# Windowed attention and a tanh-shrink MLP on one core: a new order of loads, gates set tile by tile, and global-row copies for the freer engine

## The chip, the core and the metric

The kernel runs on one core of a Trainium2 chip. The core has a matrix engine (TensorE, PE in the profile), a vector engine (VectorE, DVE), an activation engine (ScalarE, ACT), a general engine (GpSimd, POOL) and a sync engine (SyncE, SP). Each works through its own list of instructions in order; semaphores hold an instruction back until what it needs is there. Transfers between memories are issued by POOL, SP or ACT and carried out by sixteen transfer engines. The metric is the device time of one execution in microseconds (us).

## The reference

Inputs are q, k, v of shape (4, 8, 768, 64) and two weights, `moe_w_in` (512, 2048) and `moe_w_out` (2048, 512), all float32.

```
scores = q @ k^T / sqrt(64)
keep   = (key < 8) | (0 <= query - key < 96)
bias   = -slope[h] * (96 if global and not local else |query - key|)
a      = softmax(where(keep, scores + bias, -1e9))
x      = (a @ v), heads put side by side     -> (3072, 512)
h      = x @ w_in
out    = (h - tanh(h)) @ w_out               -> (3072, 512)
```

So each query sees at most 96 keys behind it and the first 8 keys of its batch, the global rows.

## The kernel before

**Tiles.** The 3072 rows are 24 units u of 128 rows, six to a batch. A unit needs the keys of its own block and of the block before it (`blocks(u)`), so the eight global rows lie outside these for units 2 to 5 of a batch. The kernel copies the global rows of K and V over the first eight rows of the preceding block's tile (rows that the window doesn't reach): `a_K` copies 8 columns of the transposed K tile, `a_V` 8 rows of the V tile. In the kernel before, VectorE makes all of these copies.

**Steps of a unit.** Load q and k (`lq`, `lk`) and v (`lv`); transpose q and k: on PE for u below 8 (`T`, then copies `Te` out of PSUM), by a transposing DMA on SP from u = 8 on (also `T`); scores `S` (PE); exp `E` (ACT); mask by multiplication `M` (DVE); `AV` (PE); division by the sum `R` (DVE); transpose of the result, `X` and `Xe`, again on PE below 8 and by SP's DMA above.

**Groups of the MLP.** Units 0 and 1 are groups of their own, the others go in pairs (2, 3), (4, 5) and so on, 13 groups g. `m1(g, f)` multiplies blocks of 128 columns of w_in, from block f on, with the group's transposed activations: four blocks for a single, two for a pair, so that a task fills one PSUM bank. `th` is the tanh on ACT, `g` the subtraction on DVE. The second layer is `m2` for units 0 to 3. For the pairs from unit 4 on, the product of two row blocks with two halves of w_out is made with seven products `p` in place of eight, on sums and differences of the inputs (`wm`, `gm`); `kp` and `jn` copy and add the results, `st` stores them.

**Weights.** w_in comes in five loads, in0 to in4, that end at column blocks 2, 4, 8, 12 and 16 (`in_end`), each in a tile of its own, w_in_bf0 to w_in_bf4. w_out comes in four loads, out0 to out3.

**What sets the order.** The kernel first writes down every step as a task with its engine (or engines: the freer one at that moment gets it), an estimated duration, what it must come after, the buffers it takes and gives, and a priority. A small planner (`Plan.run`) plays this through and yields each engine's order; only then the instructions are written in that order. The semaphores are set afterwards from the data that each instruction really reads and writes, not from the planner's list. `NUDGE` holds additions to the priorities of single tasks. `order` is a string that gives the order of the loads on POOL's queue; each load is planned after the one before it. `AHEAD` and `T_AHEAD`, both 6.0, are gates: `S(u)` and `T(u)` may not be planned before the MLP tasks have come to within six units of u. For m1 the planner's list has these lines:

```python
op(("m1", g, f), PE, ..., after=[("Xe", u) for u in us] + [("in", in_of[f + m - 1]), ...
# in m1: for f in range(f0, f0 + m): j = in_of[f]; ... w_in_bf[j] ...
```

In the profile of before, L517 is m1's matmul, L589 a product, L542 m2, L449 S, L475 AV, L405 and L417 the transposes of q and k, L495 that of the result, L369 the bias, L871 warming matmuls on zeros; L388 and L391 load q, k and v, L394 loads w_in, L397 w_out; L605 stores.

Of the kernel before, what the change touches and what calls it, by code (L numbers as in the profile page):

```python
# [11 lines left out]
ALU = mybir.AluOpType  # L12
# [186 lines left out]
def kernel(  # L199
# [41 lines left out]
    WM_PRI = 40  # L241

    groups = [[u] for u in range(SINGLE)] + [[u, u + 1] for u in range(SINGLE, NU, 2)]
    group_of = {u: g for g, us in enumerate(groups) for u in us}
    seven = [g for g, us in enumerate(groups) if SEVEN[0] <= us[0] < SEVEN[1]]
# [35 lines left out]
    buffers("pr", 5, [P, H, P], BF16)  # L281
    buffers("x", 3, [P, H, Dh], BF16)
    buffers("xT", 4, [P, CD, 2 * P], BF16)
    buffers("th", 4, [P, 512], FP32)
    buffers("g", 4, [P, CF, 2 * P], BF16)
# [5 lines left out]
    def buf(holder, j=0):  # L291
# [23 lines left out]
    def slot(h):  # L315
        return (h % 2) * NP + h // 2
# [137 lines left out]
    def a_E(u, o):  # L454
        d = buf(("p", u, o)).rearrange("k (a h) f -> k a (h f)", a=2)
        nc.scalar.activation(d, banks(("s", u), 2 * o, 2 * o + 1), AF.Exp, bias=0.0, scale=scale)  # L456

    def a_M(u, o):
        t = buf(("p", u, o))
        nc.vector.tensor_tensor(out=t, in0=t, in1=mk[:, mask_of(u, o)], op=ALU.mult)  # L460
# [10 lines left out]
    def a_AV(u):  # L471
        t = av(u)
        for h in range(H):
            for o in blocks(u):
                nc.tensor.matmul(  # L475
                    t[:, h // (H // 2), h % (H // 2), :], buf(("p", u, o))[:, slot(h), :], buf(("v", u - o))[:, h, :],
                    start=o == 0, stop=o == blocks(u)[-1],
                )
# [30 lines left out]
    def m1(g, f0, m):  # L509
        n = len(groups[g]) * P  # L510
        t = bank(("h", g, f0))
        x = buf(("xT", g))
        for f in range(f0, f0 + m):
            j = in_of[f]
            fo = (f - in_from[j]) * P
            for c in range(CD):
                nc.tensor.matmul(  # L517
                    t[:, (f - f0) * n : (f - f0 + 1) * n], w_in_bf[j][:, c, fo : fo + P], x[:, c, 0:n],
                    start=(c == 0), stop=(c == CD - 1),
                )  # L520
# [4 lines left out]

    def m1_th(g, f0, m):
        nc.scalar.activation(  # L527
            h_view(buf(("th", g, f0)), g, m), h_view(bank(("h", g, f0)), g, m), AF.Tanh, bias=0.0, scale=1.0
        )

    def m1_g(g, f0, m):
        n = len(groups[g]) * P
        nc.vector.tensor_tensor(  # L533
            out=buf(("g", g))[:, f0 : f0 + m, 0:n], in0=h_view(bank(("h", g, f0)), g, m),
            in1=h_view(buf(("th", g, f0)), g, m), op=ALU.subtract,
        )

    def m2(u, part, fs, c0, c1):
        g = group_of[u]
        t = groups[g].index(u)  # L540
        for f in fs:
            nc.tensor.matmul(  # L542
                bank(part)[:, 0 : c1 - c0], buf(("g", g))[:, f, t * P : (t + 1) * P],
                w_out_bf[:, f, c0:c1], start=(f == 0), stop=(f == CF - 1),
            )
# [20 lines left out]
    def w_mixes(i):  # L566
        t = [w_mix[:, n] for n in range(4)]
        if i == 0:
            sub(t[0], w_half(0, 1), w_half(0, 0))
        elif i == 1:  # L570
            sub(t[1], w_half(1, 1), t[0])
        elif i == 2:
            sub(t[2], w_half(1, 1), w_half(0, 1))
        else:
            sub(t[3], w_half(1, 0), t[1])
# [46 lines left out]
    T_AHEAD = 6.0  # L622
# [23 lines left out]
    for u in range(HW):  # L646
# [16 lines left out]
    )  # L663
    ring = [(x.rstrip("0123456789"), int(x.lstrip("kqvinout"))) for x in order.split()]
    prev = None
    for kind, u in ring:
        if kind == "v":
# [14 lines left out]
        elif kind == "in":  # L682
            load(("in", u), POOL, 0.75, lambda e, u=u: load_w_in(e, u), W_WT * (in_end[u] - in_from[u]) / 4, prev, pri=-40)
            prev = ("in", u)
        else:
            load(("out", u), POOL, 0.75, lambda e, u=u: load_w_out(e, u), W_WT, prev, pri=-40)
            prev = ("out", u)

# [3 lines left out]
    for g, us in enumerate(groups):  # L692
        m = 4 // len(us)
        units[g] = [(f, m) for f in range(0, CF, m)]
        for f, m in units[g]:
            prog.append((acc, ("m1", g, f)))
            acc += len(us) * m / CF

    FLEX = (ACT, DVE)
    for u in range(NU):  # L700
# [3 lines left out]
        go = [key for a, key in prog if a <= u - AHEAD]  # L704
        here = [("ck", u), ("cq", u)] if u < HW else [("lk", u), ("lq", u)]
        first = [key for a, key in prog if a <= u - T_AHEAD]
        tdep = here + [("issue", first[-1]) if first else None]
        sdep = [("issue", go[-1])] if go else []
# [26 lines left out]
        for o in blocks(u):  # L735
            op(("E", u, o), ACT, 1.03, lambda e, u=u, o=o: a_E(u, o), after=[("S", u)],
               take=[(("p", u, o), "pr", 1)], give=[(("s", u), (2 * o, 2 * o + 1))], pri=base)
            if u >= BIASED:
# [8 lines left out]
        a_give = [(("p", u, o), None) for o in blocks(u)]  # L747
# [23 lines left out]
    for g, us in enumerate(groups):  # L771
        n = len(us) * P
        for f, m in units[g]:
# [4 lines left out]
               take=[(("h", g, f), "bank", 1)], pri=pri,  # L778
# [3 lines left out]
               take=[(("th", g, f), "th", 1)], pri=pri)  # L782
            op(("g", g, f), DVE, 0.15 + 1.07 * w, lambda e, g=g, f=f, m=m: m1_g(g, f, m),
               after=[("th", g, f), ("issue", ("g", g, 0)) if f else None],
               take=[(("g", g), "g", 1)] if f == 0 else [], give=[(("h", g, f), None), (("th", g, f), None)], pri=pri)
# [8 lines left out]
    for i in range(4):  # L794
        op(("wm", i), DVE, 0.15 + 2048 / 1920, lambda e, i=i: w_mixes(i),
           after=[("out", j) for j in range(WJ)] + ([("wm", i - 1)] if i in (1, 3) else []) + ([("wm", 1)] if i == 3 else []), pri=WM_PRI)
    for g, us in enumerate(groups):
        if g not in seven:
            continue
        u0, u1 = us  # L800
        pri = 1030 + 10.0 * u0
        done = [("g", g, f) for f, m in units[g]]
# [13 lines left out]
        prod(6, sa, lambda g=g: mix(g, 1), lambda: w_mix[:, 1], False, [("gm", g, 1), ("wm", 1), ("kp", g, 0)], [], mg)  # L816
        prod(5, sb, lambda g=g: mix(g, 0), lambda: w_mix[:, 0], True, [("gm", g, 0), ("wm", 0), ("jn", g, 0)], [], mg)
        prod(7, sa, lambda g=g: mix(g, 2), lambda: w_mix[:, 2], False, [("gm", g, 2), ("wm", 2), ("kp", g, 1)], [], mg)
        prod(4, sa, lambda g=g: g_half(g, 1, 1), lambda: w_mix[:, 3], False, [("wm", 3), ("kp", g, 2)], [], gg)
# [19 lines left out]
    for u in range(NU):  # L839
        g = group_of[u]  # L840
        if g in seven:
            continue
# [3 lines left out]
        for c0, c1 in cols:  # L846
            part = ("o", u, c0)
            steps = [range(4 * a, 4 * a + 4) for a in range(4)] if c1 - c0 == DM else [range(CF)]
            for a, fs in enumerate(steps):
                op(("m2", u, c0, a), PE, len(fs) * ((c1 - c0) / 2400.0 + 0.0025),  # L850
                   lambda e, u=u, part=part, fs=fs, c0=c0, c1=c1: m2(u, part, fs, c0, c1),
                   after=[("out", fs[-1] // FJ), ("issue", prev) if prev else None] + [("g", g, f) for f in sorted({f // m * m for f in fs})],
                   take=[(part, "bank", 1)] if a == 0 else [],
                   give=[(("g", g), None)] if a == len(steps) - 1 else [],
# [6 lines left out]
            wait = ("p", group_of[u + 1], 1) if u + 1 < NU and group_of[u + 1] in seven else ("m2", u + 1, 0, 2)  # L861
# [61 lines left out]
```

## Time and profile before

| | before |
|---|---|
| time, median of 3 runs | 209.36 us (208.21 to 210.05) |
| profiled execution, first to last instruction (its span) | 207.0 us |
| PE busy | 200.6 us, 97% |
| DVE busy | 164.7 us, 80% |
| ACT busy | 123.4 us, 60% |
| POOL busy | 79.6 us, 38% |
| mean granted clock of PE | 0.997 |
| moved by the transfer engines | 26.85 MB |

The span runs from the first to the last instruction of one profiled execution; for that execution no other time is recorded, so its own time is this span and what lies around it, and the median of the runs is 2.4 us above the span. Busy time is the time in which an engine has an instruction under way. Idle time matters only on the engine that others wait for. A row of groups gives line, engine, operation, tiles, shapes and count, then busy time and the mean of one in ns, then the idle time just before and what ended it.

### The profile page before, as it was taken

What the parts mean: (1) busy time and instruction counts of PE and PEld (TensorE: products, weight loads), DVE (VectorE), ACT (ScalarE), POOL (GpSimd) and SP (SyncE); (2) the same over time, 40 slices, a digit from 0 to 9 for tenths busy, and PEclk for the clock granted to TensorE, in tenths of its full rate; (3) what the DMA queues carried; (4) which work ended last, traced back from release to release, by engine and by line L of the source; (5) the groups of instructions that cost most, each with busy time, mean ns of one, the idle gap of its engine ahead of it and who ended that gap; (6) DMA issues with size and microseconds to landing.
All of it is one profiled execution on the core that took longest, in us unless ns stands there. A gap on an engine that the chain in (4) does not pass through costs nothing.

```text
span 207.0 us, 5642 instructions
## 1 busy us (share of the span) xinstructions
PE 200.6 (97%) x2303; PEld 165.9 (80%) x2303; DVE 164.7 (80%) x336; ACT 123.4 (60%) x194; POOL 79.6 (38%) x105
## 2 busy tenths in 40 slices
PE   5998999999999998999999999999999999999993
PEld 1568987758668887888889888888898898888883
DVE  5339995898689897898988998888899889775761
ACT  3698966456747685556577545756656745545320
POOL 7997336498465543536391732002101020000030
PEclk9999999999999999999999999999999999999998
DMA  5999999999999999999999999922462022000052
GB/s 134 148 168 197 207 190 189 177 157 145 133 157 190 147 181 113 167 166 157 119 213 131 233 119 157 189 48 101 85 139 63 0 76 79 0 3 0 3 209 98
DMA packets 101514, 26.85 MB, mean 130 GB/s; under 512 B 92848, under 2 KB 100016, under 8 KB 101488
## 3 DMA queue, kind: packets, MB, share of 16 engines
q0 software_dynamic: 74624, 18.88, 94.9%
q1 hardware_dynamic: 26592, 7.34, 26.5%
q8 instruction: 18, 0.29, 0.6%
q10 hardware_dynamic: 272, 0.26, 0.5%
q14 instruction: 8, 0.07, 0.1%
HBM read 27.26 MB, written 6.29 MB: 162 GB/s over the span
## 4 chain that ended last, share of the span: by engine, by line
PE 91%; DMA 4%; DVE 2%; POOL 1%; issue 1%; POOLq 0%; DVEq 0%
PE ps L517 38%; PE ps L589 29%; PE ps L542 7%; PE ps L449 6%; PE ps L475 5%; DMA xT<-x 4%; PE ps L369 2%; PE ps L417 1%; PE ps L495 1%; PE ps L405 1%; DVE x L484 1%; DVE slopes L359 0%; PE ps L413 0%; POOL kq L388 0%; DVE ot L596 0%
## 5 line engine op out<-in xcount | busy, mean ns | idle before, releaser
L517 PE MATMUL ps<-xT,w_in_bf 128*128 128x256 bf16 (+1 forms) x832 | 92.8, 264 | 0.6 <-DMA xT<-x 0.6
L517 PEld LDWEIGHTS <-w_in_bf 128*128 128x128 bf16 x832 | 74.8, 98 | 9.5 <-issue 0.8
L527 ACT ACTIVATE th<-ps 128x512 f32<-128x512 f32 x96 | 56.9, 600 | 42.4 <-PE ps L517 39.3
L533 DVE TENSOR_TENSOR g<-ps,th 128x512 bf16<-128x512 f32 x96 | 62.8, 682 | 8.5 <-ACT th L527 7.8
L456 ACT ACTIVATE pr<-ps 128x1024 bf16<-128x1024 f32 x44 | 43.5, 1027 | 6.3 <-PE ps L449 6.2
L605 POOL DMA_DIRECT2D out_dram<-ot x21 | 11.8, 562 | 78.8 <-DVE ot L596 36.3
L589 PEld LDWEIGHTS <-mix 128*128 128x128 bf16 x320 | 30.7, 98 | 4.1
L589 PE MATMUL ps<-w_mix,mix 128*128 128x256 bf16 x240 | 29.7, 273 | 0.0
L460 DVE TENSOR_TENSOR pr<-pr,mk 128x1024 bf16<-128x1024 bf16 x39 | 26.2, 681 | 1.9 <-ACT pr L456 1.7
L589 PEld LDWEIGHTS <-g 128*128 128x128 bf16 x240 | 22.9, 98 | 3.3
L391 POOL DMA_DIRECT2D vb<-in_v_dram x24 | 21.3, 894 | 10.4 <-DVE pr L460 3.6
L391 POOL DMA_DIRECT2D kq<-in_k_dram x20 | 17.8, 888 | 17.2 <-DMA qk<-kq 9.1
L391 POOL DMA_DIRECT2D kq<-in_q_dram x20 | 17.8, 888 | 6.9 <-DMA kq<-in_q_dram 2.7
L589 PE MATMUL ps<-w_out_bf,g 128*128 128x256 bf16 x160 | 20.0, 273 | 0.0
L596 DVE TENSOR_TENSOR ot<-ps,part 128x256 f32<-128x256 f32 x30 | 12.7, 422 | 7.5 <-PE ps L589 5.3
L323 ACT COPY part<-ps 128x256 f32<-128x256 f32 x25 | 9.3, 372 | 15.3 <-PE ps L589 15.2
L484 DVE TENSOR_TENSOR x<-ps,rden 128x512 bf16<-128x512 f32 x24 | 16.6, 692 | 0.8
L542 PE MATMUL ps<-w_out_bf,g 128*128 128x512 bf16 x64 | 16.0, 379 | 0.0
L475 PE MATMUL ps<-vb,pr 128*128 128x65 bf16 x352 | 14.6, 193 | 0.0
L475 PEld LDWEIGHTS <-pr 128*128 128x128 bf16 x352 | 13.7, 97 | 1.0
L449 PEld LDWEIGHTS <-qk 64*128 64x128 bf16 x352 | 9.9, 94 | 5.4 <-issue 4.6
L564 DVE TENSOR_TENSOR mix<-g 128x1024 bf16<-128x1024 bf16 x20 | 13.6, 681 | 0.0
(57 smaller groups left out, 147.7 us busy)
## 6 DMA issues: line engine op xcount, KB each, us to landing
out_dram<-ot POOLq DMA_DIRECT2D x21, 256.0 KB, 6.4
vb<-in_v_dram POOLq DMA_DIRECT2D x24, 128.0 KB, 11.1
kq<-in_k_dram POOLq DMA_DIRECT2D x23, 128.0 KB, 9.9
kq<-in_q_dram POOLq DMA_DIRECT2D x23, 128.0 KB, 10.2
w_out_bf<-in_moe_w_out_dram POOLq DMA_DIRECT2D x4, 512.0 KB, 14.0
w_in_bf<-in_moe_w_in_dram POOLq DMA_DIRECT2D x3, 512.0 KB, 9.6
w_in_bf<-in_moe_w_in_dram POOLq DMA_DIRECT2D x2, 256.0 KB, 6.2
out_dram<-ot SPq DMA_DIRECT2D x4, 128.0 KB, 1.7
```

Of the source, the lines that this page charges most:

```text
L391: eng(e).dma_start(out=dst, in_=rows_of(src, u).rearrange("h p d -> p h d"))
L449: nc.tensor.matmul(bank(("s", u), 2 * o + hh)[:, p * P : (p + 1) * P], buf(("qk", u - o))[r, 1, p, :], buf(("qk", u))[r, 0, p, :], start=u ...
L456: nc.scalar.activation(d, banks(("s", u), 2 * o, 2 * o + 1), AF.Exp, bias=0.0, scale=scale)
L460: nc.vector.tensor_tensor(out=t, in0=t, in1=mk[:, mask_of(u, o)], op=ALU.mult)
L475: nc.tensor.matmul(t[:, h // (H // 2), h % (H // 2), :], buf(("p", u, o))[:, slot(h), :], buf(("v", u - o))[:, h, :], start=o == 0, stop=o ...
L484: nc.vector.tensor_tensor(out=buf(("x", u)).rearrange("q (a h) d -> q a h d", a=2), in0=t[:, :, :, 0:Dh], in1=rden.to_broadcast([P, 2, H / ...
L517: nc.tensor.matmul(t[:, (f - f0) * n : (f - f0 + 1) * n], w_in_bf[j][:, c, fo : fo + P], x[:, c, 0:n], start=(c == 0), stop=(c == CD - 1),)
L527: nc.scalar.activation(h_view(buf(("th", g, f0)), g, m), h_view(bank(("h", g, f0)), g, m), AF.Tanh, bias=0.0, scale=1.0)
L533: nc.vector.tensor_tensor(out=buf(("g", g))[:, f0 : f0 + m, 0:n], in0=h_view(bank(("h", g, f0)), g, m), in1=h_view(buf(("th", g, f0)), g, ...
L542: nc.tensor.matmul(bank(part)[:, 0 : c1 - c0], buf(("g", g))[:, f, t * P : (t + 1) * P], w_out_bf[:, f, c0:c1], start=(f == 0), stop=(f == ...
L564: nc.vector.tensor_tensor(out=out, in0=a, in1=b, op=op)
L589: nc.tensor.matmul(bank(part)[:, 0:NH], a[:, j], w[:, j], start=first and j == 0, stop=j == CF // 2 - 1, skip_group_check=not first)
```

## The change

The computation stays the same. What changes:

- `COPIES = (DVE, ACT)`: the planner may give each `K` and `V` copy to VectorE or to ScalarE.
- `GATE`: the number of units by which `S(u)` and `T(u)` keep behind the MLP is given for each u from 6 on, in place of 6.0 for all.
- `order`: the loads are put in a new order; among others in1, in3 and in4 come ahead of in0, and in2 after it.
- `NUDGE`: some 60 priorities become about 190.
- Tasks of the product pairs are numbered by u // 2; tiles `pr` have one more dimension of size 1. Some switches are new and off (`WIDE`, `JOINED`, `WH = 1`) and change nothing.

```diff
+    COPIES = (DVE, ACT)
...
     NUDGE = {
-        ('rel',): 850, ('dist',): 2630, ('lq', 1): 4260, ('lk', 12): 1980, ('S', 0): 910, ('AV', 0): 2360,
...
+        ('rel',): 850, ('dist',): -1670, ('first',): 1500, ('turn',): 4500, ('bm', 0): -2100, ('ck', 0): 7100,
...
-    T_AHEAD = 6.0
+    GATE = {
+        ('T', 6): 3.5, ('S', 6): 3.5, ('T', 7): 1.25, ('S', 7): 2.25, ('T', 8): 3, ('S', 8): 5.25, ('T', 9): 4.5,
...
     order = (
-        "kq1 kq2 in0 v0 v1 v2 kq3 v3 kq4 in1 in2 in3 in4 out0 kq5 out1 v4 v5 out2 out3 kq6 v6 kq7 kq8 "
-        "kq9 v7 v8 v9 kq10 v10 kq11 kq12 v11 v12 v13 kq13 kq14 v14 v15 kq15 kq16 v16 kq17 v17 kq18 "
-        "v18 kq19 v19 kq20 v20 kq21 kq22 v21 v22 v23 kq23 "
+        "kq1 v0 kq3 kq2 v1 in1 in3 v3 v2 in4 kq5 in0 kq4 in2 out1 out0 v4 kq6 out2 out3 kq7 v5 kq8 v7 v6 kq9 "
+        "kq10 v23 kq12 kq11 v8 v10 v9 v16 v12 kq14 v13 kq13 kq15 v11 kq20 kq16 v19 v14 v18 v21 kq22 v15 v22 "
+        "kq17 v20 kq23 v17 kq18 kq21 kq19 "
     )
...
-        go = [key for a, key in prog if a <= u - AHEAD]
+        ga = sum(a <= GATE.get(("S", u), u - AHEAD) for a, _ in prog) - 1
+        gt = sum(a <= GATE.get(("T", u), u - AHEAD) for a, _ in prog) - 1
...
-            op(("K", u), DVE, 0.16, lambda e, u=u: a_K(e, u), after=[("S", u)],
+            op(("K", u), COPIES, 0.17, lambda e, u=u: a_K(e, u), us2=0.25, after=[("S", u)],
-            op(("V", u), DVE, 0.3, lambda e, u=u: a_V(e, u), after=[("AV", u)],
+            op(("V", u), COPIES, 0.3, lambda e, u=u: a_V(e, u), us2=0.62, after=[("AV", u)],
```

In the program that comes of it, the first tasks on PE are, before: bm1, B0, bm2, T0, bm0, T1, T2, S0, B1, S1, B2, S2, AV0, AV1, T3, X1, X0, AV2, S3, T4, X2, m1(0, 0), m1(1, 0); after: bm1, bm0, B0, bm2, T0, T1, S0, B1, S1, AV0, T3, T2, X0, B2, AV1, S2, m1(0, 0), X1, S3, m1(0, 8), m1(1, 0), AV2.

More of the change, by code (lines that the diff above doesn't have):

```diff
@@ L241 @@
     WM_PRI = 40
+    WH = 1
+    WIDE = {}
+    COPIES = (DVE, ACT)
+    JOINED = False
     groups = [[u] for u in range(SINGLE)] + [[u, u + 1] for u in range(SINGLE, NU, 2)]
     group_of = {u: g for g, us in enumerate(groups) for u in us}
-    seven = [g for g, us in enumerate(groups) if SEVEN[0] <= us[0] < SEVEN[1]]
+    seven = [w for w in range(NU // 2) if SEVEN[0] <= 2 * w < SEVEN[1]]
     pool = ctx.enter_context(tc.tile_pool(name="sb", bufs=1))
@@ L533, in m1_g @@
         nc.vector.tensor_tensor(
-            out=buf(("g", g))[:, f0 : f0 + m, 0:n], in0=h_view(bank(("h", g, f0)), g, m),
+            out=g_cols(groups[g][0], n)[:, f0 : f0 + m], in0=h_banks(g, f0, m),
             in1=h_view(buf(("th", g, f0)), g, m), op=ALU.subtract,
@@ L564, in sub, with w_mixes @@
         nc.vector.tensor_tensor(out=out, in0=a, in1=b, op=op)
-    def w_mixes(i):
-        t = [w_mix[:, n] for n in range(4)]
+    def w_mixes(i, j):
+        c = slice(j * CF // (2 * WH), (j + 1) * CF // (2 * WH))
+        t = [w_mix[:, n, c] for n in range(4)]
         if i == 0:
-            sub(t[0], w_half(0, 1), w_half(0, 0))
+            sub(t[0], w_half(0, 1)[:, c], w_half(0, 0)[:, c])
         elif i == 1:
-            sub(t[1], w_half(1, 1), t[0])
+            sub(t[1], w_half(1, 1)[:, c], t[0])
         elif i == 2:
-            sub(t[2], w_half(1, 1), w_half(0, 1))
+            sub(t[2], w_half(1, 1)[:, c], w_half(0, 1)[:, c])
         else:
-            sub(t[3], w_half(1, 0), t[1])
+            sub(t[3], w_half(1, 0)[:, c], t[1])
     def g_mixes(g, i):
@@ L665 @@
     prev = None
+    plan.chain = []
     for kind, u in ring:
+        first = len(plan.ops)
         if kind == "v":
@@ L687 @@
             prev = ("out", u)
+        plan.chain.append(list(plan.ops)[first:])
     units = {}
@@ L692 @@
     for g, us in enumerate(groups):
-        m = 4 // len(us)
-        units[g] = [(f, m) for f in range(0, CF, m)]
+        sizes = WIDE.get(g, [4 // len(us)] * (CF * len(us) // 4))
+        units[g] = [(sum(sizes[:i]), m) for i, m in enumerate(sizes)]
         for f, m in units[g]:
@@ L697 @@
             acc += len(us) * m / CF
-    FLEX = (ACT, DVE)
+    plan.prog = [key for a, key in prog]
+    plan.accs = [a for a, key in prog]
+    plan.gates = {}
     for u in range(NU):
@@ L703 @@
         base = 10.0 * u
-        go = [key for a, key in prog if a <= u - AHEAD]
+        ga = sum(a <= GATE.get(("S", u), u - AHEAD) for a, _ in prog) - 1
+        gt = sum(a <= GATE.get(("T", u), u - AHEAD) for a, _ in prog) - 1
         here = [("ck", u), ("cq", u)] if u < HW else [("lk", u), ("lq", u)]
-        first = [key for a, key in prog if a <= u - T_AHEAD]
-        tdep = here + [("issue", first[-1]) if first else None]
-        sdep = [("issue", go[-1])] if go else []
+        tdep = here + [("issue", prog[gt][1]) if gt >= 0 else None]
+        sdep = [("issue", prog[ga][1])] if ga >= 0 else []
+        if gt >= 0:
+            plan.gates["T", u] = gt
+        if ga >= 0:
+            plan.gates["S", u] = ga
         kq_give = [(("kq", u), None)]
@@ L735 @@
         for o in blocks(u):
-            op(("E", u, o), ACT, 1.03, lambda e, u=u, o=o: a_E(u, o), after=[("S", u)],
-               take=[(("p", u, o), "pr", 1)], give=[(("s", u), (2 * o, 2 * o + 1))], pri=base)
-            if u >= BIASED:
+            op(("E", u, o), ACT, 1.03, lambda e, u=u, o=o: a_E(u, o), after=[("S", u)] + ([("issue", ("E", u, 0))] if JOINED and o else []),
+               take=[] if JOINED and o else [(("p", u), "pr", 1)] if JOINED else [(("p", u, o), "pr", 1)],
+               give=[(("s", u), (2 * o, 2 * o + 1))], pri=base)
+            if u >= BIASED and JOINED and nb == 2:
+                if o:
+                    op(("M", u), DVE, 1.22, lambda e, u=u: a_M2(u),
+                       after=[("E", u, 0), ("E", u, 1), ("em", 1), ("em", 2)], pri=base)
+            elif u >= BIASED:
                 op(("M", u, o), DVE, 0.71, lambda e, u=u, o=o: a_M(u, o),
@@ L794, with wmd @@
     for i in range(4):
[L795 to L800, printed above, removed]
+        for j in range(WH):
+            op(("wm", i, j), DVE, 0.15 + 2048 / WH / 1920, lambda e, i=i, j=j: w_mixes(i, j),
+               after=[("out", n) for n in range(j * WJ // WH, (j + 1) * WJ // WH)]
+               + ([("wm", i - 1, j)] if i in (1, 3) else []) + ([("wm", 1, j)] if i == 3 else []), pri=WM_PRI)
+    def wmd(i):
+        return [("wm", i, j) for j in range(WH)]
+    for g in seven:
+        u0, u1 = 2 * g, 2 * g + 1
         pri = 1030 + 10.0 * u0
-        done = [("g", g, f) for f, m in units[g]]
+        done = [("g", h, f) for h in sorted({group_of[u0], group_of[u1]}) for f, m in units[h]]
         for i in range(4):
@@ L840 @@
         g = group_of[u]
-        if g in seven:
+        if u // 2 in seven:
             continue
@@ L851 @@
                    lambda e, u=u, part=part, fs=fs, c0=c0, c1=c1: m2(u, part, fs, c0, c1),
-                   after=[("out", fs[-1] // FJ), ("issue", prev) if prev else None] + [("g", g, f) for f in sorted({f // m * m for f in fs})],
+                   after=[("out", fs[-1] // FJ), ("issue", prev) if prev else None] + [("g", g, f) for f, m in units[g] if f <= fs[-1] and f + m > fs[0]],
                    take=[(part, "bank", 1)] if a == 0 else [],
-                   give=[(("g", g), None)] if a == len(steps) - 1 else [],
+                   give=[(("g", u // 2), None)] if a == len(steps) - 1 else [],
                    pri=1030 + 10.0 * u)
```

55 lines of the change are left out of this document (35 added, 20 removed), and 45 rows, old and new, of tables (GATE, NUDGE).

## The prediction

> **What bounds the kernel now.** I read the page first: busy times, the slices, the queues.
>
> ```profile
> span 207.0 us, 5642 instructions
> PE 200.6 (97%) x2303; PEld 165.9 (80%) x2303; DVE 164.7 (80%) x336; ACT 123.4 (60%) x194; POOL 79.6 (38%) x105
> ...
> DMA  5999999999999999999999999922462022000052
> ...
> q0 software_dynamic: 74624, 18.88, 94.9%
> ```
>
> TensorE (PE) is busy for 97% of the span. The transfer engines are full from the second slice to the twenty-sixth, about 134 us: POOL's queue q0 always has a backlog there. A busy PE need not be a PE at work, so next the busy time by stretch: the start, the stretch from the first matmul of the first MLP layer on, and the end.
>
> ```profile
> 4.80:19.40 14.60, 13.99 (x189) 9.28 (x190) 7.67 (x30) 11.31 (x14) 14.29 (x18) 1.00 1.69 168
> 19.40:203.90 184.50, 183.83 (x2112) 155.93 (x2108) 154.40 (x294) 110.19 (x179) 61.72 (x79) 1.00 1.22 127
> 203.90:207.00 3.10, 0.00 (x0) 0.00 (x0) 0.39 (x1) 0.00 (x0) 0.00 (x0) 0.82 0.25 85
> ```
>
> The columns are length, then PE, PEld, DVE, ACT and POOL busy, clock, DMA share, GB/s. From 19.4 us to 203.9 us PE lacks 0.7 us of 184.5; behind it lie 3.1 us, the last sum and stores. The table of waits names the 0.6 us of it, one wait for a transposed activation:
>
> ```profile
> PE ps L517 <- DMA xT<-x: 0.6, 1, 0.6
> ```
>
> So the kernel is PE from end to end. A reordering can win back little, since each matmul stays; what it can do is make PE wait, and then the end moves by the whole wait. The question for each part is therefore: what does PE now wait for that it did not?
>
> **The change part by part.** *The order of the loads.* The old order issues the five pieces of w_in as in0, in1, in2, in3, in4; the new one issues in1, in3, v3, v2, in4, kq5, in0, kq4, in2. Piece in0 holds column blocks 0 and 1, in1 blocks 2 and 3. The planner lets the task m1(g, f) wait for the piece of its last block alone (`in_of[f + m - 1]`). For the single groups m is 4, so m1(0, 0) multiplies with blocks 0 to 3 and needs in0 and in1, but is planned on in1 only. In the old order that is harmless, since in0 lands first. In the new program m1(0, 0) is the 17th task on PE, its first weight load reads in0, and in0 is the 16th load on POOL's queue. The real semaphore is there whatever the planner thinks, and PE works strictly in its order: all of PE stands until in0 has landed.
>
> When does it land? POOL's issues of before (start, length), and the loads' times from issue to landing:
>
> ```profile
> 9.54 0.89 POOL L391 DMA_DIRECT2D vb<-in_v_dram  x1
> ...
> 11.28 0.89 POOL L391 DMA_DIRECT2D kq<-in_q_dram  x1
> 12.15 1.61 POOL L394 DMA_DIRECT2D w_in_bf<-in_moe_w_in_dram  x2
> 13.92 1.48 POOL L394 DMA_DIRECT2D w_in_bf<-in_moe_w_in_dram  x2 [0.15 <-issue]
> 15.38 0.76 POOL L397 DMA_DIRECT2D w_out_bf<-in_moe_w_out_dram  x1
> ...
> 17.01 0.89 POOL L391 DMA_DIRECT2D kq<-in_q_dram  x1
> ```
>
> ```profile
> kq<-in_k_dram POOLq DMA_DIRECT2D x1, 128.0 KB, 4.1
> ...
> vb<-in_v_dram POOLq DMA_DIRECT2D x1, 128.0 KB, 6.0
> ...
> kq<-in_q_dram POOLq DMA_DIRECT2D x1, 128.0 KB, 5.8
> ...
> w_in_bf<-in_moe_w_in_dram POOLq DMA_DIRECT2D x1, 256.0 KB, 6.3
> ...
> w_in_bf<-in_moe_w_in_dram POOLq DMA_DIRECT2D x1, 512.0 KB, 8.0
> ...
> w_out_bf<-in_moe_w_out_dram POOLq DMA_DIRECT2D x1, 512.0 KB, 14.0
> ...
> kq<-in_q_dram POOLq DMA_DIRECT2D x1, 128.0 KB, 14.0
> ```
>
> ```profile
> DMA to landing us min/median/max: 6.0/8.0/12.1
> ```
>
> The first of these lists is POOL's timeline, the second the list of issues, asked around single ones in the order of issue (the first is the very first load, on an empty queue), the third the answer on the five w_in loads: in0, the first, has the shortest time, in4, the last, the longest. Issue and landing added: v3 (9.5) is in at 15.5, q4 (11.3) at 17.1, in1 (12.15) at 18.4, in2 (13.0, the second of its row) at 21.0, in4 (14.65, the second of its row) at 26.7, the first piece of w_out (15.4) at 29.4, q5 (17.0) at 31.0. The issues are 0.9 us apart and the time to landing grows from 6 to 14 us: the loads come in one behind the other, in the order of issue, and what a load costs is the step to the one before it: in2 2.6, k4 with q4 1.6, k5 with q5 1.6.
>
> In the old order 17 loads end with in4, at 26.7. In the new one 16 loads end with in0: the same without in2 and kq4, and with kq5. So in0 lands at 26.7 - 2.6 - 1.6 + 1.6 = 24.1 us; I take 24.2, for the iota that now stands ahead of the first load (below). The bounds: 18.0 us if in0 needed only the very first load's 4.1 us after the 16th issue, which began at 13.9 in the old order; 25.5 if the iota's whole time and a slower mix shift it. The growing landing times speak for the queue, near the upper end.
>
> A sentence of the Trainium skill speaks for the lower end: "DMA: Bandwidth & Descriptors", section "Anatomy of one DMA — SWDGE (gpsimd) path", gives 2.0 us plus the bytes over 436 GB/s. By it the 3.1 MB that these 16 loads write would be in an estimated 9.2 us after the first issue, PE would not wait at all, and the sum would stay near 207. The rows differ: in2's 512 KB took 2.6 us, about 200 GB/s, and the rows decide.
>
> *When PE gets there, and how much is behind.* Old PE work ahead of m1(0, 0) that the new order puts behind it: X1, AV2, S3, T4, X2. From the chain of work (start, length):
>
> ```profile
> 17.11 0.55 PE ps L495 x8
> 17.67 0.48 PE ps L475 x16
> 18.15 0.55 PE ps L449 x16
> 18.71 0.55 PE ps L405 x8
> 19.26 0.32 PE ps L495 x4
> ```
>
> Half of the first row, and the other four: 2.2 us. So PE reaches m1(0, 0) at 19.4 - 2.2 = 17.2 us at the latest, and waits some 7 us; it can be 15, if the constants come earlier. How early does not matter. From the landing on PE has the old 184.5 us (the 0.6 us wait left in) plus 2.2: 24.2 + 184.5 + 2.2 = 210.9 us.
>
> *The clock.* The trace has PE idle for long only at its end, and cold only at its start:
>
> ```profile
> 200.00:205.80 5.80, 3.82 (x36) 3.18 (x33) 1.27 (x3) 0.74 (x2) 0.00 (x0) 1.00 0.45 159
> 205.90:207.00 1.10, 0.00 (x0) 0.00 (x0) 0.00 (x0) 0.00 (x0) 0.00 (x0) 0.50 0.00 0
> ```
>
> ```profile
> 4.88 2.74 PE ps L369 x6
> ...
> 8.92 0.43 PE ps L369 x2
> ```
>
> ```profile
> L871 PE MATMUL ps<-zero 128*128 128x512 bf16 x7 | 3.4, 627 | 1.0 <-DVE vb L365 1.0
> ```
>
> The granted clock falls from 1.00 to 0.50 about 2 us after the last matmul. At the start the 512-column matmul takes 0.46 us at 4.9 us and 0.22 at 8.9: PE's first, warming matmuls had begun after 1.0 us of idling, so the half clock lasts about 7 us. A wait of 7 us is over three times the 2 us, so I expect the clock to fall and matmuls to go at half speed after the wait. That costs half of the slow time: 0 if the clock does not fall, 3.5 if all 7 us come again. I take 2.4, nearer the upper end, as at the start PE was also idle for part of the time. The Trainium skill says the same in "TensorE: Matmul & The Clock Gate", "What's actually happening": half clock after an idle window of 3.4 us, full again after a busy one; with free-running windows that is 3.4 to 6.8 slow us, an estimated loss of 1.7 to 3.4.
>
> *Copies of the global rows.* Counting the new order, 14 of the 16 V copies and 5 of the 16 K copies go to ScalarE.
>
> ```profile
> L325 DVE COPY vb<-vb 8x512 bf16<-8x512 bf16 x16 | 6.1, 380 | 0.8 <-PE ps L475 0.8
> L325 DVE COPY qk<-qk 128x32 bf16<-128x32 bf16 x16 | 3.3, 208 | 3.3 <-PE ps L449 3.3
> L323 ACT COPY part<-ps 128x256 f32<-128x256 f32 x25 | 9.3, 372 | 15.3 <-PE ps L589 15.2
> L323 ACT COPY xT<-ps 128x512 bf16<-128x512 bf16 x5 | 2.9, 587 | 1.4 <-PE ps L495 1.4
> ```
>
> VectorE loses 14 x 0.38 + 5 x 0.21 = 6.4 us. ScalarE gains 19 copies; this copy has no row there, so 0.2 (VectorE's K copy) to 0.59 each, 4 to 11 us; I take 0.5, as 512 elements a row is the V copy's form, about 9 us on 123. Neither is on the path: PE lacks 0.7 us in all, so relief on VectorE buys nothing, and ScalarE is idle 40% of the span. With that cover gone, an exp or tanh behind a copy is 0.5 us late, and so may PE be: 0 to +2 over the kernel; I take 0.
>
> *Gates, priorities, later loads.* The same matmuls in another order: 0 by itself. Eight matmuls of m1 or of a product take 0.87 us:
>
> ```profile
> 85.15 1.75 PE ps L589 x16
> 86.90 1.75 PE ps L517 x16
> ```
>
> By these, S's 0.55 and AV's 0.48 I counted along both orders the PE work between the last AV of a pair and its first m1, which must hide the SP transposes: for g = 5, where the 0.6 us wait was, it goes from 8.8 to 8.4 us, so the wait may be 1.0; for g = 9 from 10.3 to 7.6, for g = 11 from 18.7 to 8.0. Between S and the AV of the same u it stays at 4.4 us or more from u = 4 on. Loads have 7 us more lead on a PE that is late. -0.6 to +2; I take 0. The two warming matmuls fewer and the constants (iota ahead of the first load, dist ahead of slopes) move PE's start, which the wait swallows.
>
> *The end.* The stores of rows 20 and 21 come two products ahead of the end instead of six. From the list of issues:
>
> ```profile
> out_dram<-ot POOLq DMA_DIRECT2D x21, 256.0 KB, 6.4
> ...
> out_dram<-ot SPq DMA_DIRECT2D x1, 256.0 KB, 3.7
> ```
>
> Store 20, on POOL, is issued about 1.2 us ahead of PE's end. At SP's 3.7 us it lands 2.5 after it, inside the 3.1; at the median 6.4, which has the loads beside it, 5.2 after it: 0 to +2.1; I take 0, as the loads are done by then.
>
> *The sum.* 210.9 + 2.4 = 213.3 for PE's end, + 3.1 = 216.4 us of span against 207.0: +9.4. The runs' median, 209.36, lies 2.4 us above that span, which I keep: 218.8 us.
>
> **The rivals.** (1) The wait comes, but the clock stays up. For it: nothing in the trace shows a fall followed by work. Against: the 0.50 after 2 us of idling. 216.4 us. (2) The wait comes and more follows: late exps behind copies, transposes with less cover, the last POOL store. For it: the shorter covers for g = 9 and 11. Against: PE was fed without a gap with covers as short. With the upper ends (+2, +2, and half the cold time more), 221 to 224 us. (3) Not slower: loads on the queue do not wait for each other, and in0 lands as the first load on an empty queue does, 4.1 us after its issue, at 18.0. PE waits 1 to 3 us, the clock stays: 18.0 + 184.5 + 2.2 + 3.1 + 2.4 = 210.2 us, within 1% of before. It decides from a landing at 19.2 us or earlier (211.4 us). For it: in0 took 6.0 us in the old order with four loads ahead, not much more than 4.1. Against: the growing landing times. (4) The change does not do what it says, because PE is not really held at m1(0, 0): only if in0's weight load stood later; the program's order has it first.
>
> **How the numbers follow.** Forecast 0.74; (1) 0.10; (2) 0.12; (3) 0.03; (4) 0.01. The forecast's own range, with in0 from 23.7 to 25 and the clock term from 1.5 to 3.4, is 217.4 to 220.6. With (1) below, its landing as uncertain, and most of (2) above: 215.0 to 223.3. A measurement of this kernel tells about 1% from no change, 2.1 us. Slower by more than that: forecast, (1), (2), 0.96; within it: most of (3) and (4), 0.03; faster 0.01.
>
> **What would show it.** In the new profile PE has one gap of 6 to 9 us ahead of its first w_in matmul, at about 16 to 24 us, put down to the load of w_in; the in0 load lands near 24 us; matmuls after it take twice their time for some us; from there to PE's end about 189 us; VectorE about 6 us less busy, ScalarE about 9 more. The prediction is wrong if the first w_in matmul starts before 19 us, or if later gaps on PE add up to more than 3 us.

## The result and the profile after

The changed kernel takes 217.68 us (median of four runs, 217.06 to 217.99), the kernel before in the same session 209.52 us (208.21 to 210.05): a ratio of 1.0399, with a 95% interval of 1.0362 to 1.0436. It is 4% slower. The forecast was 218.8 us. Ratios leave out single runs that lie more than 1.5% above the fastest of their kernel, of the experiments below one of e1's twelve runs and three of e10's.

The page of the profiled execution after: span, busy times, and the rows of slices for TensorE, its granted clock and the transfer engines.

```profile
span 215.8 us, 5619 instructions
...
PE 200.6 (93%) x2295; PEld 166.7 (77%) x2301; DVE 161.2 (75%) x316; ACT 131.7 (61%) x214; POOL 79.8 (37%) x105
...
PE   7960399999999999999999999999999999999993
...
PEclk9997589999999999999999999999999999999999
DMA  6999999999999976999999999943203221001024
```

TensorE's busy time is that of before to the tenth, 200.6 us (a coincidence: 4.1 us of it, behind the hole, are at half clock), but the span is 8.8 us longer. The hole is in slices three to five (each is 5.4 us long), in which the transfer engines stay full, and the clock row falls in it and stays low up to slice six. Behind slice five TensorE's row is full up to the end. So there is one event, and the waits and TensorE's timeline name it. A row of waits gives who waits, for what, the sum in us, how often and the longest; a row of a timeline gives start, length, engine, line, operation, tiles, shapes, count, and the idle time before it with its releaser.

```profile
PE ps L552 <- DMA w_in_bf<-in_moe_w_in_dram: 9.9, 1, 9.9
...
PE ps L509 <- DMA vb<-in_v_dram: 0.5, 1, 0.5
```

```profile
14.68 0.39 PE L476 MATMUL ps<-qk,qk 64*128 64x128 bf16 x8
24.93 1.89 PE L552 MATMUL ps<-xT,w_in_bf 128*128 128x128 bf16 x16 [9.87 <-DMA w_in_bf<-in_moe_w_in_dram]
...
28.14 2.36 PE L552 MATMUL ps<-xT,w_in_bf 128*128 128x128 bf16 x32
...
30.83 1.05 PE L552 MATMUL ps<-xT,w_in_bf 128*128 128x128 bf16 x16
```

L552 is m1's matmul in the new line numbers. TensorE finishes the scores of unit 2 at about 15.05 us and stands for 9.87 us. Sixteen of m1's matmuls take 1.89 us right behind the wait and 1.05 us six microseconds later: half clock, then full clock. Two more views name the load. The first row is from the chain of work (start, length), the second from POOL's timeline:

```profile
14.09 10.79 DMA w_in_bf<-in_moe_w_in_dram
```

```profile
14.09 0.76 POOL L421 DMA_DIRECT2D w_in_bf<-in_moe_w_in_dram  x1 [0.64 <-DMA vb<-in_v_dram]
```

The load issued at 14.09 is in0, the sixteenth on POOL's queue. It is in at 24.88 us, 10.79 us after its issue, and TensorE starts 0.05 us later. By stretch (limits and length in us, then busy time and count of PE, PEld, DVE, ACT and POOL, clock, DMA share, GB/s):

```profile
15.05:18.70 3.65, 0.01 (x2) 0.00 (x0) 0.52 (x2) 1.91 (x3) 1.44 (x2) 1.00 1.77 182
...
18.80:29.00 10.20, 4.07 (x45) 3.68 (x46) 0.91 (x3) 1.11 (x2) 6.58 (x9) 0.50 1.66 188
...
24.93:212.47 187.54, 187.27 (x2151) 159.16 (x2156) 152.28 (x276) 119.50 (x199) 60.70 (x78) 0.99 1.07 119
212.47:215.80 3.33, 0.00 (x0) 0.00 (x0) 0.00 (x0) 0.37 (x1) 0.00 (x0) 1.00 0.45 158
```

The clock falls 3.7 us into the wait and is back at about 29.0 us, 4.1 us after TensorE has begun again. From the landing to TensorE's end it lacks only 0.27 us of 187.54, and the tail is 3.3 us. The copies of the global rows, in the list of groups:

```profile
L350 ACT COPY vb<-vb 8x512 bf16<-8x512 bf16 x14 | 8.6, 612 | 5.7 <-PE ps L509 5.6
...
L352 DVE COPY qk<-qk 128x32 bf16<-128x32 bf16 x11 | 2.7, 248 | 1.2 <-PE ps L476 1.1
...
L350 ACT COPY qk<-qk 128x32 bf16<-128x32 bf16 x5 | 1.1, 210 | 0.0
...
L352 DVE COPY vb<-vb 8x512 bf16<-8x512 bf16 x2 | 0.6, 282 | 1.6 <-PE ps L509 1.6
```

Fourteen V copies and five K copies went to ScalarE, 9.7 us in all; nothing in TensorE's waits names one of them.

### The profile page after: what moved, and what is told of

Its sections match the earlier page's. It is cut to its first block, busy times and chain, and to the rows that moved or that the text cites. A ratio compares the mean times of both kernels' runs of the same rounds, so it can differ in the third digit from the quotient of the medians.

```text
span 215.8 us, 5619 instructions
## 1 busy us (share of the span) xinstructions
PE 200.6 (93%) x2295; PEld 166.7 (77%) x2301; DVE 161.2 (75%) x316; ACT 131.7 (61%) x214; POOL 79.8 (37%) x105
## 4 chain that ended last, share of the span: by engine, by line
PE 87%; DMA 8%; POOL 3%; issue 0%; ACT 0%; POOLq 0%
PE ps L552 40%; PE ps L632 29%; PE ps L584 6%; PE ps L476 5%; DMA w_in_bf<-in_moe_w_in_dram 5%; PE ps L509 5%; DMA vb<-in_v_dram 3%; POOL kq L415 2%; PE ps L529 1%; PE ps L432 1%; POOL vb L418 0%; ACT ot L350 0%; POOL rel L356 0%; POOLq L356 0%; POOLq L973 0%
## 5 line engine op out<-in xcount | busy, mean ns | idle before, releaser
L552 PE MATMUL ps<-xT,w_in_bf 128*128 128x256 bf16 (+1 forms) x832 | 91.8, 267 | 9.9 <-DMA w_in_bf<-in_moe_w_in_dram 9.9
L552 PEld LDWEIGHTS <-w_in_bf 128*128 128x128 bf16 x832 | 76.4, 99 | 18.4 <-DMA w_in_bf<-in_moe_w_in_dram 10.0
L577 DVE TENSOR_TENSOR g<-ps,th 128x512 bf16<-128x512 f32 x96 | 63.5, 685 | 8.8 <-ACT th L568 7.2
L584 PE MATMUL ps<-w_out_bf,g 128*128 128x512 bf16 x59 | 14.9, 379 | 0.3
L476 PEld LDWEIGHTS <-qk 64*128 64x128 bf16 x352 | 10.2, 96 | 5.6 <-issue 5.5
```

The lines of the kernel that those rows point to most:

```text
L476: nc.tensor.matmul(bank(("s", u), 2 * o + hh)[:, p * P : (p + 1) * P], buf(("qk", u - o))[r, 1, p, :], buf(("qk", u))[r, 0, p, :], start=u ...
L552: nc.tensor.matmul(t[:, o % 512 : o % 512 + n], w_in_bf[j][:, c, fo : fo + P], x[:, c, 0:n], start=(c == 0), stop=(c == CD - 1),)
L577: nc.vector.tensor_tensor(out=g_cols(groups[g][0], n)[:, f0 : f0 + m], in0=h_banks(g, f0, m), in1=h_view(buf(("th", g, f0)), g, m), op=ALU ...
L584: nc.tensor.matmul(bank(part)[:, 0 : c1 - c0], g_cols(u)[:, f], w_out_bf[:, f, c0:c1], start=(f == 0), stop=(f == CF - 1),)
```

## The experiments

The theory: nearly all of the loss is in0's place on POOL's queue, the wait itself and the clock that falls in it; gates, priorities, copies and the later loads cost nothing that can be seen. The edits below act on the planner's finished order, or add matmuls while it is written out (e3, e9), so that what is not named stays where it was. `move(a, b, dt)` gives task a the planned time of task b plus dt: right ahead of it or right behind it on its engine.

**In0 to the front (e1).** In the changed kernel one load is moved, from behind kq5 to just ahead of in1.

```diff
     order, start, got, end = plan.run(free)
     holds.update(got)
+    move(("in", 0), ("in", 1), -1e-4)
```

> The changed kernel with one load moved: in0 is issued just ahead of in1; every other instruction stands on its engine as in the changed kernel. Theory (the 9.9 us wait for in0 is the whole loss): in0 lands near 15 us, PE then waits only in small steps for in1 (16.4), in3 (18.9) and in4 (23.2), the clock stays up, PE ends near 203.7 us, span 207, time 209 us (207.5 to 211), no slower than before within 1%. Rival (the new gates, priorities and ScalarE copies cost the time, and the wait only hides it): the gap goes and others come later, the time stays at 215 us or more.

Measured: 208.0 us, ratio to before 0.9946 (0.9918 to 0.9974). The span, two rows of TensorE's waits and one of its timeline:

```profile
span 205.8 us, 5626 instructions
```

```profile
PE ps L552 <- DMA w_in_bf<-in_moe_w_in_dram: 1.1, 1, 1.1
...
PE ps L476 <- DMA qk<-kq: 0.4, 1, 0.4
```

```profile
14.67 1.07 PE L552 MATMUL ps<-xT,w_in_bf 128*128 128x128 bf16 x16
```

One load's place takes back the whole loss, and a little more: everything else of the change together, with in0 in this place, is worth about half a per cent in the kernel's favour. The first m1 matmul starts at 14.67 us at full speed. What is left is 1.1 us for in3, which m1(0, 8) needs, and 0.4 us for a transposed tile.

**The same fault put into the kernel before (e2).** Here the load is moved behind in4, its seventeenth place.

```diff
     order, start, got, end = plan.run(free)
     holds.update(got)
+    move(("in", 0), ("in", 4), 1e-4)
```

> The kernel before with one load moved: in0 is issued right behind in4, all else as before. Theory: in0 lands near 26.7 us (the same bytes ahead of it as ahead of the end of in4 before), PE waits some 7.3 us ahead of its first w_in matmul, the clock falls for about 4 us (2 us lost), span 207 + 9.4, time 218.5 us (216.5 to 220.5). Rival (the loss comes from the other parts of the change, which are not in this kernel): within 1% of before, 207.5 to 211.5 us.

Measured: 217.16 us, ratio 1.0381 (1.0334 to 1.0427). Its wait, its timeline and the stretch at half clock:

```profile
PE ps L517 <- DMA w_in_bf<-in_moe_w_in_dram: 8.5, 1, 8.5
```

```profile
26.94 3.59 PE L517 MATMUL ps<-xT,w_in_bf 128*128 128x128 bf16 x32 [8.50 <-DMA w_in_bf<-in_moe_w_in_dram]
```

```profile
21.40:31.60 10.20, 4.66 (x50) 4.27 (x51) 1.18 (x3) 1.62 (x3) 4.22 (x6) 0.50 1.47 197
```

With none of the change's other parts, the late load alone makes the kernel before 3.8% slower. The load landed where a seventeenth load was forecast to (26.7; here 26.90, and TensorE starts at 26.94). The wait is 8.5 us rather than the 7.3 expected, because TensorE was at m1 1 us earlier than in the profiled execution of the kernel before: the first six bias matmuls, from 4.9 us on in both, took 1.74 us here and 2.74 us there. The change has no part in this.

**The wait without the cold clock (e3).** The changed kernel with 42 matmuls on zeros ahead of m1(0, 0), whose result is overwritten: the wait stays, but TensorE is at work in it.

```diff
...
+                if key == ("m1", 0, 0):
+                    for _ in range(42):
+                        nc.tensor.matmul(
+                            bank(("h", 0, 0)), zero[:, 0, :], zero.to_broadcast([P, 4, P]), start=True, stop=True
+                        )
```

> The changed kernel with 42 more matmuls of 512 columns on zeros ahead of m1(0, 0), into the PSUM bank that this task takes: 42 x 0.216 = 9.1 us of the 9.9 us wait are filled, and m1(0, 0) still begins when in0 lands. Theory (the wait lets the clock fall, and the half clock from 24.9 to 29.0 us costs 2 us): the clock stays up, time 215.7 us (214.8 to 216.5). Rival (the slow matmuls behind the wait cost nothing at the end, because other engines would hold PE there anyway): 217.7 us, as the changed kernel, or a little more.

Measured: 215.13 us, ratio 1.0273 (1.0219 to 1.0326). TensorE's timeline, and the stretch from the landing to its end:

```profile
14.70 9.24 PE L958 MATMUL ps<-zero 128*128 128x512 bf16 x42
25.21 1.07 PE L552 MATMUL ps<-xT,w_in_bf 128*128 128x128 bf16 x16 [1.28 <-DMA w_in_bf<-in_moe_w_in_dram]
```

```profile
25.21:211.00 185.79, 185.75 (x2156) 157.58 (x2156) 152.25 (x276) 119.49 (x199) 60.72 (x78) 1.00 1.10 119
```

Behind a wait filled with work the same matmuls take 185.79 us in place of 187.54: the clock's fall costs 1.75 us by these two rows (1.52 us of it is busy time, 0.23 us idle time), 2.05 us by half of the 4.1 slow us. By the medians it is 2.55 us, 217.68 against 215.13; the profiled execution of e3 was the slowest of its four. The rest of the loss stays. The load of in0 was issued 0.69 us earlier here than in the changed kernel (13.40 against 14.09) and landed 0.28 us later: an earlier issue at the same place in the queue brought nothing.

**All copies on VectorE (e4).** The kernel of e1, with every K and V copy on VectorE at its place in time.

```diff
...
+    order[:] = [(t, k, DVE if k[0] in ("K", "V") else e) for t, k, e in order]
```

> The first kernel of this series (in0 ahead of in1) with all K and V copies on VectorE again, at the places in time where they stand in the changed kernel's order. Theory (the copies lie beside PE): VectorE about 6 us busier, ScalarE about 9 less, time the same as with the copies on ScalarE within 0.5%. Rival A (copies on ScalarE make exps and tanhs late): 1 to 2 us faster. Rival B (the relief of VectorE is worth something): 1 to 3 us slower.

Measured: 207.78 us, ratio 0.9955 (0.9918 to 0.9991), the same as e1. Busy times, and the two groups of copies:

```profile
PE 199.9 (97%) x2301; PEld 165.2 (80%) x2301; DVE 164.9 (80%) x335; ACT 123.7 (60%) x195; POOL 79.7 (39%) x105
```

```profile
L352 DVE COPY vb<-vb 8x512 bf16<-8x512 bf16 x16 | 5.4, 339 | 4.8 <-PE ps L509 4.8
L352 DVE COPY qk<-qk 128x32 bf16<-128x32 bf16 x16 | 3.1, 194 | 1.0 <-PE ps L476 0.9
```

The place of the copies has no effect on the time that 12 runs can show. The sixteen V copies take 339 ns each here, by their mean, against 612 ns for one on ScalarE.

**In0 a little late (e5).** The changed kernel with in0 right behind in3, so that the wait is short.

```diff
     order, start, got, end = plan.run(free)
     holds.update(got)
+    move(("in", 0), ("in", 3), 1e-4)
```

> The changed kernel with in0 issued right behind in3, half way between its place there and the place ahead of in1; all else as in the changed kernel. Theory (the end follows in0's landing one for one, plus the clock): in0 lands near 19.0 us (in3's 17.6 and 1.4 for its own 256 KB), PE waits from 15.0, 4.0 us; the later small wait for in3 falls away; PE ends near 205.4 us, span 208.7, time 211 us (210 to 212) if 4 us are too short for the clock to fall, 213 if it falls. Rival (the time depends on the order of tasks, not on the landing): 215 us or more, as the changed kernel, or 208, as with in0 first.

Measured: 211.85 us, ratio 1.0123 (1.0077 to 1.0169), between the two expectations. The number alone would have been taken for the first, in which the clock stays up (210 to 212); the trace shows that it fell, behind a wait that was shorter than the 4.0 us expected. The wait in TensorE's timeline, and four stretches:

```profile
18.43 1.89 PE L552 MATMUL ps<-xT,w_in_bf 128*128 128x128 bf16 x16 [3.10 <-DMA w_in_bf<-in_moe_w_in_dram]
```

```profile
15.30:17.30 2.00, 0.03 (x2) 0.00 (x0) 0.54 (x2) 1.92 (x3) 0.75 (x1) 1.00 1.71 183
17.40:24.10 6.70, 5.67 (x60) 5.28 (x61) 1.98 (x4) 1.94 (x2) 3.39 (x6) 0.50 1.96 175
...
18.43:207.56 189.13, 188.47 (x2156) 159.66 (x2156) 152.22 (x276) 119.45 (x199) 64.67 (x82) 0.98 1.20 124
```

A wait of 3.1 us, a third of the other, lets the clock fall after some 2 us of idling, and TensorE then works at half speed from 18.43 to about 24.1 us. Half of these 5.7 us is 2.8 us: in this execution the short wait costs nearly as much again in speed, and more than the 9.9 us wait did. It was the slowest of the four, with a mean granted clock of 0.984; the other three show 0.992, which makes an estimated 3.4 us at half clock in place of 6.7 (0.8% of some 210 us is 1.7 us lost, and half clock lasts twice that), so there the clock cost 1.7 us at most.

**The short wait filled (e9).** To see whether that loss is the clock, the kernel of e5 with 13 of the matmuls on zeros ahead of m1(0, 0).

```diff
...
+                if key == ("m1", 0, 0):
+                    for _ in range(13):
+                        nc.tensor.matmul(
+                            bank(("h", 0, 0)), zero[:, 0, :], zero.to_broadcast([P, 4, P]), start=True, stop=True
+                        )
```

> The kernel of e5_in0_after_in3 (in0's load right behind in3's), with 13 matmuls of 512 columns on zeros ahead of m1(0,0) on TensorE, which fill 2.8 of its 3.1 us of waiting; their results are not used. Theory: what e5 lost beyond its wait is the clock, which fell although the wait was only 3.1 us; with TensorE busy through it the clock stays up to the end of the stage, TensorE ends 2.9 us earlier than in e5, and the time is about 209 us (208.2 to 210). Rival: the slow stretch of e5 was hidden by waits that would have come anyway; then the time stays at 211.9 and the end of TensorE at 207.6 us.

Measured: 208.95 us, ratio 0.9987 (0.9965 to 1.001). What is left of the wait, and the stretch from the landing to TensorE's end:

```profile
PE ps L552 <- DMA w_in_bf<-in_moe_w_in_dram: 1.2, 1, 1.2
```

```profile
18.27:203.95 185.68, 185.65 (x2156) 157.34 (x2156) 151.99 (x276) 119.46 (x199) 64.67 (x83) 1.00 1.19 126
```

The same matmuls take 185.68 us in place of 189.13, of which 2.8 us are busy time (188.47 to 185.65) and 0.6 us idle time that goes too. TensorE ends 3.6 us earlier, 0.2 us of it because the load landed earlier. Matmuls whose results nobody reads make the kernel 1.4% faster (1.0123 to 0.9987), 2.9 us by the medians. The mean clock is 0.997 or more in all ten executions. The rival, that other waits would hide the slow matmuls, is out.

**The rest of the hole filled (e6, e10).** In e1 TensorE still waits 1.1 us for in3 while m1(1, 0) stands ready behind. In e6 four tasks are turned to m1(1, 0), m1(0, 8), m1(1, 8), AV2; `places` gives the index of a task in `order`, and in0 is moved as in e1.

```diff
...
+    line = [("m1", 0, 8), ("m1", 1, 0), ("AV", 2), ("m1", 1, 8)]
+    times = [order[places[k]][0] for k in line]
+    for t, k in zip(times, [("m1", 1, 0), ("m1", 0, 8), ("m1", 1, 8), ("AV", 2)]):
+        order[places[k]] = (t, k, PE)
```

> The kernel with in0 ahead of in1, and on PE the four tasks m1(0, 8), m1(1, 0), AV2, m1(1, 8) in the order m1(1, 0), m1(0, 8), m1(1, 8), AV2: m1(1, 0) needs only in0 and in1 and stands in the 1.1 us wait for in3. Theory (PE has no slack, so each wait at the start moves the end): the wait for in3 shrinks below 0.3 us, PE ends 0.9 us earlier, time 207.1 us (206 to 208.2). Rival (the wait comes back a little later, at v2 or in4, whose transfers stand in the same queue): no change, 208.0 us.

Measured: 208.34 us, ratio 0.9949 (0.9919 to 0.998): no gain over e1, where 207.1 (206 to 208.2) was expected. Two of its waits, and one row of ScalarE's timeline:

```profile
PE ps L509 <- ACT vb L350: 0.6, 1, 0.6
PE ps L552 <- DMA w_in_bf<-in_moe_w_in_dram: 0.3, 1, 0.3
```

```profile
21.06 0.62 ACT L350 COPY vb<-vb 8x512 bf16<-8x512 bf16 x1 [1.76 <-PE ps L509]
```

The wait for in3 fell as intended, and a new one came: AV3 now stands right behind AV2 and needs the V copy that AV2 must let go first. In e10 that one copy goes to VectorE.

```diff
...
+    order[:] = [(t, k, DVE if k == ("V", 2) else e) for t, k, e in order]
```

> The kernel of e6_gap_filled with one edit: the copy of V's global rows of chunk 2 is on VectorE, not ScalarE. Theory: the third block of outputs, which in that order stands right behind the second, waited 0.65 us for that copy, and the copy took 0.62 us on ScalarE; at VectorE's 0.34 us the wait falls to about 0.35 us, and the time stays within 0.8 us of 208.0, so that the wait's row decides and not the time. Rival: the wait is for something that the copy only accompanies (the landing of v, or the hand-over between the engines), and stays at 0.6 us.

Measured: 208.2 us, ratio 0.9936 (0.991 to 0.9963). The same wait, and the copy in VectorE's timeline:

```profile
PE ps L509 <- DVE vb L352: 0.4, 1, 0.4
```

```profile
20.75 0.41 DVE L352 COPY vb<-vb 8x512 bf16<-8x512 bf16 x1 [1.57 <-PE ps L509]
```

The copy is 0.21 us shorter, and in the timelines the idle time ahead of AV3 falls from 0.65 to 0.44 us: the wait is the copy. It is the only wait of TensorE for such a copy in the tables of waits of all runs. The times of e1, e4, e6 and e10 can't be told from each other.

**The early constants alone (e8).** In the kernel before, the iota is put ahead of the first load and the distances ahead of the slopes. `turned(new, old)` gives the planned times of the tasks `old`, earliest first, to the tasks `new`.

```diff
...
+    turned([("rel",), ("lk", 1)], [("lk", 1), ("rel",)])
+    dve = [("slopes",), ("turn",), ("dist",), ("ident",), ("first",), ("ones", 1)]
+    turned([("dist",), ("slopes",), ("first",), ("turn",), ("ident",), ("ones", 1)], dve)
```

> The kernel before with the start of the changed one alone: the iota ahead of the first load on POOL, the mask distances ahead of the slopes on VectorE; all else as before. Theory (what the kernel with in0 first gains over before comes from its earlier start, 14.7 us instead of 17.2 for the same work): the first bias matmul starts at 3.7 us instead of 4.9, PE reaches its first w_in matmul about 0.9 us earlier, in1 (18.5 us) just covers it, span 206.2, time 208.4 us (207.6 to 209.2). Rival (the gain comes from gates and priorities later on): 209.0 us as before, within 0.2%.

Measured: 208.59 us, ratio 0.9977 (0.995 to 1.0005). Its first bias matmul, and its wait for w_in:

```profile
3.53 2.61 PE L369 MATMUL ps<-slopes,dist 128*128 128x512 bf16 x6
```

```profile
PE ps L517 <- DMA w_in_bf<-in_moe_w_in_dram: 1.3, 2, 0.8
```

The bias begins 1.35 us earlier than in the kernel before (3.53 against 4.88), but TensorE now runs into pieces of w_in that land no earlier and gives most of it back. Whether this part alone gains anything stays open, as the interval takes in 1; so does how the half per cent of e1 divides between the early start and the new order of loads.

## Why the prediction was right, step by step

- **Which load, and when it lands.** The planner knows m1(0, 0) as waiting for in1 only, while the data need in0; that was the main step, and e1 and e2 show it from both sides. The landing was put at 24.2 us and came at 24.88: counting steps between loads of one queue held to 0.7 us. By the prediction's estimate from the Trainium skill ("DMA: Bandwidth & Descriptors", "Anatomy of one DMA — SWDGE (gpsimd) path") the sixteenth load would not have been late at all; the trace decides against that here, where the queue has a backlog and one load took 10.79 us.
- **The wait.** TensorE reached m1(0, 0) at about 15.05 us, at the early end of what was left open, so the gap is 9.87 us and not 6 to 9. As said there, this moves nothing: the end hangs on the landing alone.
- **The work behind it.** 184.5 + 2.2 = 186.7 us was forecast; 187.54 less 2.05 for the clock is 185.5, and 185.7 to 185.8 at full clock in e3 and e9. The term was 0.9 to 1.2 us too long. The 0.6 us wait for a transposed activation, left in it, is gone: TensorE lacks only 0.04 us behind the landing in e3 and 0.03 in e9. The other 0.3 to 0.4 us is busy time (183.83 + 2.2 = 186.0 forecast, 185.75 and 185.65 measured), and its cause stays open.
- **The clock.** 2.4 us was forecast, 2.05 measured by the slow stretch, 1.75 by the traces of e3 and 2.55 by its median. That it falls and is felt, against rival (1), is shown by e3 and e9.
- **The tail and the last stores.** 3.1 forecast, 3.3 measured; the stores of rows 20 and 21 cost nothing.
- **The copies.** VectorE became 3.5 us less busy (164.7 to 161.2), not 6.4; ScalarE 8.3 us busier, 9 forecast. For VectorE the step took rows of groups as if they added up to busy time; they do not. The rows of all its groups add up to 178.0 us before and 173.3 after, 13.3 and 12.1 us more than its busy time, so records overlap. The copies' rows fell by 6.1 us, the other rows grew by 1.4, and 1.2 us of the rest was overlap. In e4 the copies' rows are 5.4 us more than in e1 and the busy time 3.0 us. For ScalarE the V copy is 612 ns, above the upper bound of 590, and the K copy 210. That neither touches the time, e4 confirms.
- **Gates, priorities, later loads.** Costed at nothing within -0.6 and +2. Beside the wait for in0 there is 0.5 us for a v tile, ahead of the landing and swallowed by it; behind it TensorE lacks 0.27 us in all. Rival (2) has no evidence. With in0 in place, the rest of the change is the half per cent of e1.
- **What lies around the span.** The forecast kept 2.4 us, the median of the runs of before less one execution's span. After, the profiled execution took 217.56 us with its span of 215.8: 1.8 us. This term was 0.6 us too long, because a median was set beside a span of another execution.
- **The sum.** The span came 0.6 us below the 216.4 forecast: landing +0.7, work -1.2, clock -0.35, tail +0.2. With the 0.6 us around it, this is the 1.1 us by which 218.8 was too high. That the sum came out so near is in part luck: the errors have both signs, and taken without the signs they add up to 3 us.
- **Rival (3)**, a load that is not queued, needed a landing by 19.2 us; it landed at 24.88.

## What to carry to other kernels

When loads are put in a new order, list for each consumer the loads whose data it really reads, not those that the planner was told of, and count the load's place in its queue up to the first of them: on a backlogged queue the landing is the place, and an engine that works in order waits for it whole. Where TensorE must wait for a few microseconds, give it work, or matmuls that nobody needs: behind a wait of 3.1 us the clock cost 2.8 us in the profiled execution, and filling that wait made the kernel 1.4% faster. Take out a wait only after reading what stands next on that engine, and sum up terms against the time of the same execution that they come from.

## What the runs showed that was not expected

- The half clock does not follow the length of the wait. In the traces it came 3.7 us after TensorE's last work in the changed kernel, 3.0 us after it in e2, about 2 us after it in e5 and at the end of the kernel before, and not with waits of 1.1 and 1.2 us (e1, e9); in the profiled executions a wait of 3.1 us lost 2.8 us to it, one of 9.9 us only 2.05. The Trainium skill ("TensorE: Matmul & The Clock Gate", "What's actually happening") lets it fall after an idle window of about 3.4 us. The prediction set this beside the 2 us at the end of the kernel before as if they were the same, and they are not. The slow stretches fit steps of this length (about 6.8 us in e5, 10.2 in the changed kernel and in e2), but 2 us of idling were enough twice. If one step is counted back from each fall, TensorE was at work for none of it in the changed kernel, and at its beginning for an estimated 0.5 us in e2 and 1.4 us in e5 and at the end of the kernel before. That a window which is busy only at its beginning counts as idle would explain it, and is not shown.
- With in0 in front the clock still falls now and then. Nine of the 48 executions of e1, e4, e6 and e10 show a mean granted clock of 0.989 to 0.992, among them the three slowest of e4 (about 210 us) and the three slowest of e10 (211.1 to 211.6 us). None of the 69 executions of the kernel before beside the experiments is below 0.997, nor any of e3 and e9, whose waits are filled. No trace shows one of the nine, so where the clock falls in them, and whether that is all that makes them long, stays open.
- The profile's clock column does not show the slow start. In the kernel before, this stretch holds the six bias matmuls that take 0.46 us each, and it is given as 1.00:

```profile
4.80:7.70 2.90, 2.82 (x7) 0.99 (x8) 1.09 (x15) 1.06 (x2) 2.90 (x4) 1.00 1.29 149
```

  There only the length of the matmuls tells the speed. How long this lasts differs: the same six take 2.74 us in the kernel before and 1.74 us in e2.
- A copy of 8 rows of 512 elements takes 612 ns on ScalarE and 282 to 478 ns on VectorE, by the means of the runs, while the copy of 128 rows of 32 costs about the same on both (210, and 179 to 280 ns).
